# One 8 MB load of K per head, with half of it copied on-chip to free its slot, in a decode kernel with a long KV cache

## The chip, the cores and the metric

The kernel runs on one core of a Trainium2 chip; the other cores are idle. The metric is the device time of one execution in microseconds (us), as the median of several executions.

## The reference, cut to what matters

A decode step for two sequences: attention with 32 query heads on 4 KV heads over a cache of 32768 positions, then a small MLP. Everything is bf16.

```python
B, Sq, D = (2, 1, 1024)
Hq, Hkv, Sk, Dh = (32, 4, 32768, 128)
k = jnp.repeat(k_cache, rep, axis=1)           # k_cache, v_cache: [2, 4, 32768, 128]
v = jnp.repeat(v_cache, rep, axis=1)
scores = jnp.einsum('bhqd,bhkd->bhqk', q, k) * Dh ** (-0.5)
p = _softmax(scores, axis=-1)
o = jnp.einsum('bhqk,bhkd->bhqd', p, v)
# ... output projection wo, layernorm with modulation, MLP (w1 1024x3584, w2 3584x1024)
```

Each of the eight pairs of sequence and KV head ("a head" below, numbered 0 to 7) has 8.39 MB of K and 8.39 MB of V, read once. With the weights this makes 178 MB.

## The kernel before

PE is TensorE, PSUM the memory that its results go to here, and to evict is to copy from there to the on-chip memory that the loads fill (SBUF, 128 partitions). For each head, PE transposes K in 128x128 blocks into PSUM, VectorE and ScalarE evict these, PE multiplies them with q, a softmax over all 32768 scores follows, and only then can the product with V begin. All loads are issued by SyncE (SP) in program order. SP waits before each load until its slot in a 160 KB ring (per partition) is free.

```python
CH_ROWS = 8192          # a quarter of a head
TPC = CH_ROWS // 128    # 64 transposes per quarter, in 8 groups of 8
NCH = S // CH_ROWS      # 4 quarters
RING = 160 * 1024
EVAC_PATTERN = ("dve", "act", "dve", "act", "dve", "dve", "act", "dve")
# ...
def add_k(i, hf):       # half a head: 4 MB, 32 KB in each partition
    add(("K", i, hf), [2, TPC * D], A_k_cache[i % 2, i // 2].rearrange("(p h c t) d -> h p c (t d)", h=2, c=2, p=128)[hf], hf * 32 * KB, f"K{hf}")
def add_v(i):           # a whole head: 8 MB, 64 KB in each partition
    add(("V", i), [NCH, TPC * D], A_v_cache[i % 2, i // 2].rearrange("(p c t) d -> p c (t d)", c=NCH, p=128), 64 * KB, "V")
# ... stream of loads: wmod, wq, then for each head K half 0, K half 1, V, then wo, w1, w2
def need(*key):         # issues all loads up to this one, each after the readers of its slot
    # ...
        T.dma("sp", lambda e, dst=dst, src=cur.src: e.dma_start(dst, src), key=cur.sem, writes=[cur.reg], frees=old)
# ...
def tr(i, cc, g8):      # group g8 of quarter cc: 8 transposes, one eviction
    it = need("K", i, cc // 2)
    kt = it.view[:, cc % 2, :].rearrange("p (t d) -> p t d", d=D)
    # ... 8 x pe.transpose(psKT[g8 % 4], ...), then tensor_copy on VectorE or activation(Copy) on ScalarE
# ... for each head:
for cc in range(NCH):
    for g8 in range(TPC // 8):
        tr(i, cc, g8)
        pipe.append((i, cc, g8))
        # ...
        if len(pipe) > PIPE:
            qk(*pipe.pop(0))
# ... softmax, then pv(i, cc): the product with V; its last quarter frees V's slot
```

So the ring holds two K slots of 32 KB, one V slot of 64 KB and 32 KB that stay free during the heads. The first half of the next head's K can be loaded once half of this head's K has been transposed. The head loop is a hardware loop on PE, VectorE and ScalarE.

## Time and profile before

| | before |
|---|---|
| median of 3 runs | 419.99 us (419.98 to 420.0) |
| span of the profiled run | 418.7 us |
| moved from HBM | 178.28 MB |

The first fence has lines of the profile's page of the kernel before. The first line is busy time, share of the span and number of instructions by engine. PEclk and DMA are tenths in 40 equal slices of the span (9 is 90% or more), and GB/s is what the 16 DMA engines moved in each slice.

```profile
PE 291.0 (70%) x5183; PEld 231.3 (55%) x5183; DVE 209.6 (50%) x423; ACT 149.4 (36%) x179; POOL 6.8 (2%) x29
...
PEclk9999557986896997799589958986697889576585
DMA  9989999999999999999999999999999999899995
GB/s 373 450 380 449 448 404 493 398 406 446 441 432 429 423 451 429 419 454 457 391 435 476 407 416 448 438 438 426 438 438 426 416 460 457 377 448 428 424 427 249
DMA packets 5581, 178.42 MB, mean 426 GB/s; under 512 B 698, under 2 KB 706, under 8 KB 964
...
q8 instruction: 8, 0.13, 0.1%
...
DMA 71%; PE 24%; DVE 2%; issue 1%; ACT 1%; SPq 1%
```

DMA engines are busy in every slice, at 426 GB/s on average, and no compute engine comes near. The last line (the chain of waits that ended last) is mostly DMA. The trace's record of every DMA packet (a piece of a load that one of the 16 DMA engines moves at a time) says the same more sharply: between 20 us and 400 us the 16 engines together lack less than 0.05 us of work (the sum of their idle times, divided by 16). A 32 KB packet takes 1213 ns in the median and a 64 KB packet 2418. The latter is 27.1 GB/s on one engine, 434 GB/s on sixteen; the Trainium skill, "DMA: Bandwidth & Descriptors", section "Where 436 GB/s comes from", puts the ceiling of the path into SBUF at 435 GB/s, and this trace agrees. There is no room but in the number of bytes, in the cost per packet, and in the few us at both ends.

The next fence is the timeline of the DMA queue's issuer in the kernel before: start, time, queue, line, what was loaded (x2 is two issues merged, the second one later).

```profile
74.49 15.95 SPq L389 DMA_DIRECT2D K<-in_A_k_cache_dram  x2
102.47 0.33 SPq L389 DMA_DIRECT2D V<-in_A_v_cache_dram  x1
...
137.97 0.33 SPq L389 DMA_DIRECT2D V<-in_A_v_cache_dram  x1
...
174.92 0.33 SPq L389 DMA_DIRECT2D V<-in_A_v_cache_dram  x1
```

The V load at 102.47 us is that of head 1, into the slot that head 0's V has just left. By the packet records, the K of head 1 before it in the queue has its last byte at 110.6 us, and the first engine is through with it at 108.9. The issue leads by 6.4 us. In later heads it leads by more: that of head 3 is issued at 174.92, and the first engine is through with the K before it at 186.3.

Head 0 is slower than the others. Its PE timeline (start, time, then in brackets the idle time before and what ended it):

```profile
62.45 3.59 PE L536 MATMUL psKT<-ident,K 128*128 128x128 bf16 x32 [4.60 <-DMA K<-in_A_k_cache_dram]
...
77.35 0.22 PE L548 MATMUL psZ<-qcur,KT_sb 128*128 128x8 bf16 x3 [1.49 <-issue]
...
84.88 0.25 PE L548 MATMUL psS<-qcur,KT_sb 128*128 128x8 bf16 x4 [2.24 <-issue]
...
95.90 6.52 PE L584 MATMUL psZ<-V,E_sb 128*32 128x512 bf16 x64 [1.64 <-ACT E_sb L572]
```

K's first half is there at 62.45 us; two gaps called "issue" (PE waited for nothing that the profile knows) cost 1.49 and 2.24 us; the product with V starts at 95.90 and takes 6.5.

The windows of the same trace (columns: stretch, its length, busy time and count of PE, weight loads, VectorE, ScalarE and GpSimd, PE's clock, share of the DMA engines, GB/s):

```profile
core 0: us, PE busy (x) PEld busy (x) DVE busy (x) ACT busy (x) POOL busy (x), PEclk, DMA share, GB/s
90.00:110.00 20.00, 14.34 (x183) 9.29 (x181) 12.02 (x27) 6.86 (x9) 0.44 (x2) 0.74 1.02 437
110.00:115.00 5.00, 5.00 (x128) 5.00 (x126) 3.59 (x6) 3.45 (x4) 0.00 (x0) 1.00 0.97 419
115.00:135.00 20.00, 16.01 (x342) 13.83 (x342) 14.48 (x27) 11.47 (x15) 0.00 (x0) 0.85 0.99 428
```

And the eviction on VectorE, for its cost (busy time of the group, mean of one in ns, idle time before it):

```profile
L542 DVE COPY KT_sb<-psKT 128x1024 bf16<-128x1024 bf16 x160 | 106.7, 688 | 61.6 <-PE psKT L536 61.2
```

### The profile page before, as it was taken

The numbers are of one execution on the slowest core, as the hardware profiler recorded it, in microseconds if no ns is written. First come the engines' busy times: TensorE is split into PE (matmuls) and PEld (weight loads), VectorE is DVE, ScalarE is ACT, GpSimd is POOL, SyncE is SP. The second block draws the span as 40 slices with busy tenths as digits, with TensorE's granted clock in tenths as the row PEclk, the third lists the DMA queues.
The fourth block names the chain that finished last, engine by engine and source line by source line (L and its number), as shares of the span: only waits on it lengthen the run. The fifth ranks groups of instructions, "written<-read, shape, count | busy, mean of one in ns | idle before, by whom it ended". The sixth has DMA issues, their size and how long they took to land.

```text
span 418.7 us, 11609 instructions
## 1 busy us (share of the span) xinstructions
PE 291.0 (70%) x5183; PEld 231.3 (55%) x5183; DVE 209.6 (50%) x423; ACT 149.4 (36%) x179; POOL 6.8 (2%) x29
## 2 busy tenths in 40 slices
PE   1407449766996895699369957976995699564536
PEld 1104219762993794299149926962894399221214
DVE  1201105546677676467726664766477567620411
ACT  2000015533565364256405632643365166400100
POOL 3000000000000000000000000000000000000000
PEclk9999557986896997799589958986697889576585
DMA  9989999999999999999999999999999999899995
GB/s 373 450 380 449 448 404 493 398 406 446 441 432 429 423 451 429 419 454 457 391 435 476 407 416 448 438 438 426 438 438 426 416 460 457 377 448 428 424 427 249
DMA packets 5581, 178.42 MB, mean 426 GB/s; under 512 B 698, under 2 KB 706, under 8 KB 964
## 3 DMA queue, kind: packets, MB, share of 16 engines
q1 hardware_dynamic: 5572, 178.28, 98.8%
q8 instruction: 8, 0.13, 0.1%
q14 instruction: 1, 0.01, 0.0%
HBM read 178.28 MB, written 0.00 MB: 426 GB/s over the span
## 4 chain that ended last, share of the span: by engine, by line
DMA 71%; PE 24%; DVE 2%; issue 1%; ACT 1%; SPq 1%
DMA V<-in_A_v_cache_dram 39%; DMA wo<-in_A_wo_dram 10%; DMA K<-in_A_k_cache_dram 10%; PE psZ L584 10%; DMA w<-in_B_w_dram 9%; PE psKT L536 8%; DMA wmod<-in_w_mod_dram 4%; PE psS L548 1%; PE psZ L548 1%; PE psS L655 1%; PE psZ L729 1%; PE psZ L469 1%; ACT KT_sb L540 0%; PE psS L469 0%; DVE m1c L553 0%
## 5 line engine op out<-in xcount | busy, mean ns | idle before, releaser
L536 PE MATMUL psKT<-ident,K 128*128 128x128 bf16 x2048 | 163.1, 229 | 11.5 <-DMA K<-in_A_k_cache_dram 11.5
L540 ACT ACTIVATE KT_sb<-psKT 128x1024 bf16<-128x1024 bf16 x96 | 98.2, 1025 | 124.4 <-PE psKT L536 124.4
L542 DVE COPY KT_sb<-psKT 128x1024 bf16<-128x1024 bf16 x160 | 106.7, 688 | 61.6 <-PE psKT L536 61.2
L536 PEld LDWEIGHTS psKT<-ident,K 128*128 128x128 bf16 x2048 | 126.7, 102 | 13.0 <-DMA K<-in_A_k_cache_dram 12.7
L584 PE MATMUL psZ<-V,E_sb 128*32 128x512 bf16 x512 | 46.4, 541 | 23.2 <-DMA V<-in_A_v_cache_dram 20.0
L548 PE MATMUL psS<-qcur,KT_sb 128*128 128x8 bf16 x1024 | 44.7, 167 | 2.2 <-issue 2.2
L584 PEld LDWEIGHTS psZ<-V,E_sb 128*32 128x32 bf16 x512 | 18.7, 130 | 47.7 <-issue 38.8
L548 PE MATMUL psZ<-qcur,KT_sb 128*128 128x8 bf16 x1024 | 43.0, 167 | 2.2 <-issue 1.5
L548 PEld LDWEIGHTS psS<-qcur,KT_sb 128*128 128x128 bf16 x1024 | 40.0, 97 | 2.3 <-issue 2.3
L548 PEld LDWEIGHTS psZ<-qcur,KT_sb 128*128 128x128 bf16 x1024 | 37.9, 96 | 3.4 <-issue 1.6
L572 ACT ACTIVATE E_sb<-S_sb 128x512 bf16<-128x512 f32 x32 | 19.5, 630 | 29.6 <-DVE S_sb L570 29.6
L570 DVE TENSOR_TENSOR S_sb<-S_sb,gmb 128x512 f32<-128x512 f32 x32 | 20.0, 685 | 0.3
L576 DVE TENSOR_REDUCE rs<-E_sb 128x8 f32<-128x512 bf16 x32 | 19.7, 675 | 0.0
L469 PE MATMUL psS<-wmod,inT 128*32 128x512 bf16 x32 | 5.1, 624 | 16.2 <-DMA wmod<-in_w_mod_dram 16.2
L553 DVE TENSOR_REDUCE m1c<-psZ 128x8 f32<-128x512 f32 x16 | 11.1, 693 | 10.2 <-ACT S_sb L552 10.1
L595 DVE RECIPROCAL rinv<-psM 128x1 f32<-128x1 f32 x8 | 1.3, 168 | 27.7 <-PE psM L593 27.7
L605 PE MATMUL psM<-msum,hmat 128*128 128x128 f32 x16 | 4.2, 347 | 13.3 <-DVE msum L600 13.3
L559 PE MATMUL psM<-identf,m 128*8 128x128 f32 x16 | 4.3, 369 | 13.1 <-DVE m L556 13.1
L553 DVE TENSOR_REDUCE m1c<-psS 128x8 f32<-128x512 f32 x16 | 11.1, 693 | 3.2 <-ACT S_sb L552 3.1
L552 ACT ACTIVATE S_sb<-psZ 128x512 f32<-128x512 f32 x16 | 9.5, 595 | 7.5 <-PE psZ L548 7.5
L477 DVE COPY S_sb<-psS 128x512 f32<-128x512 f32 x1 | 0.7, 690 | 22.9 <-PE psS L469 22.9
L469 PEld LDWEIGHTS psS<-wmod,inT 128*32 128x32 bf16 x32 | 1.1, 132 | 19.3 <-DMA wmod<-in_w_mod_dram 18.0
(123 smaller groups left out, 167.5 us busy)
## 6 DMA issues: line engine op xcount, KB each, us to landing
K<-in_A_k_cache_dram SPq DMA_DIRECT2D x16, 4096.0 KB, 27.1
wq<-in_A_wq_dram SPq DMA_DIRECT2D x2, 4096.0 KB, 44.8
wo<-in_A_wo_dram SPq DMA_DIRECT2D x2, 4096.0 KB, 39.0
w<-in_B_w_dram SPq DMA_DIRECT2D x2, 3584.0 KB, 32.5
wmod<-in_w_mod_dram SPq DMA_DIRECT2D x1, 6144.0 KB, 29.8
w<-in_B_w_dram SPq DMA_DIRECT2D x3, 2048.0 KB, 37.8
wmod<-in_w_mod_dram SPq DMA_DIRECT2D x1, 4608.0 KB, 15.8
wmod<-in_w_mod_dram SPq DMA_DIRECT2D x1, 1536.0 KB, 6.0
```

The source lines that it names most:

```text
L469: pe(lambda e, w=it.view, k=k, kk=kk, ch=ch, n=n, q=q: e.matmul(bank[n][32 * q:32 * q + 32, :], lhsT=inT[:, k, :], rhs=w[:, kk, ch * 512:( ...
L536: pe(lambda e, kq=kq, jj=jj, w=kt, t=t: e.transpose(psKT[kq][:, jj * 128:(jj + 1) * 128], w[:, t, :], ident[:, :]), reads=[it.reg, "ident" ...
L540: act(lambda e, src=src: e.activation(KT_sb[g8][:, :, :], src, ACT.Copy), reads=[f"psKT{kq}"], writes=[f"KT_sb{g8}"], sem=f"ev{cc}_{g8}")
L542: dve(lambda e, src=src: e.tensor_copy(KT_sb[g8][:, :, :], src), reads=[f"psKT{kq}"], writes=[f"KT_sb{g8}"], sem=f"ev{cc}_{g8}")
L548: pe(lambda e, t=t, jj=jj: e.matmul(ps[:, t * HPG:(t + 1) * HPG], lhsT=KT_sb[g8][:, jj, :], rhs=qcur[:, :], start=True, stop=True), reads= ...
L552: act(lambda e: e.activation(Sc, ps.rearrange("p (t h) -> p h t", h=HPG), ACT.Copy), reads=[preg], writes=[f"S_sb_{cc}"], sem=f"sc{cc}")
L553: dve(lambda e: e.tensor_reduce(m1c[:, :, cc], ps.rearrange("p (t h) -> p h t", h=HPG), AX.X, ALU.max), reads=[preg], writes=[f"m1c{cc}"])
L559: pe(lambda e: e.matmul(psM[0:HPG, 0:128], lhsT=m1[:, :], rhs=identf[:, :], start=True, stop=True), reads=["m1", "identf"], writes=["psM"])
L570: dve(lambda e: e.tensor_tensor(Sc, Sc, gmb[:, :].unsqueeze(2).to_broadcast([128, HPG, TPC]), ALU.subtract), reads=[f"S_sb_{cc}", "gmb"], ...
L572: act(lambda e: e.activation(Ec, Sc.rearrange("p h (u t) -> p u h t", t=4), ACT.Exp, scale=SCALE), reads=[f"S_sb_{cc}"], writes=[f"E_sb_{c ...
L576: dve(lambda e: e.tensor_reduce(rs4[:, :, cc], Ec.rearrange("p u h t -> p h u t"), AX.XY, ALU.add), reads=[f"E_sb_{cc}"], writes=[f"rs4_{c ...
L584: pe(lambda e, t4=t4, tg=tg, q=q: e.matmul(psO[32 * q:32 * q + 32, :], lhsT=E_sb[:, tg // 4, :, :].rearrange("p h t -> p (h t)"), rhs=vt[: ...
```

## The change

The intent: K's packets become as large as V's, a single load and semaphore per head replace two, and the second half of K is copied to the spare 32 KB early in the head (with copies on VectorE, which was half idle), so that the slot is free again at half time as before. The eviction pattern shifts some work to ScalarE in the first two quarters, and the weights after the heads move within the ring.

```diff
--- before
+++ after
@@
 RING = 160 * 1024
+KC_AT = 128 * 1024
 AHEAD = ("sc2", "sc3", "pk", "ac")
 WMOD_ITEMS = ((0, 1), (1, 4), (4, 8))
-W2_ITEMS = ((0, 8, 96), (8, 16, 112), (16, 24, 128), (24, 27, 144), (27, 28, 150))
-EVAC_PATTERN = ("dve", "act", "dve", "act", "dve", "dve", "act", "dve")
+W2_ITEMS = ((0, 8, 96), (8, 16, 112), (16, 24, 0), (24, 27, 16), (27, 28, 22))
+EVAC_PATTERN = (("dve", "act") * 4, ("dve", "act", "dve", "act", "dve", "dve", "act", "dve"))
@@
-    def add_k(i, hf):
-        add(("K", i, hf), [2, TPC * D], A_k_cache[i % 2, i // 2].rearrange("(p h c t) d -> h p c (t d)", h=2, c=2, p=128)[hf], hf * 32 * KB, f"K{hf}")
+    def add_k(i):
+        add(("K", i), [NCH, TPC * D], A_k_cache[i % 2, i // 2].rearrange("(p c t) d -> p c (t d)", c=NCH, p=128), 0, "K")
@@
     for i in range(NBG):
-        add_k(i, 0)
-        add_k(i, 1)
+        add_k(i)
         add_v(i)
-    for m, off in enumerate((128, 0)):
+    for m, off in enumerate((0, 32)):
         add(("wo", m), ...)
-    for m, off in enumerate((32, 64)):
+    for m, off in enumerate((128, 64)):
         add(("w1", m), ...)
@@
+    kc = nc.alloc_sbuf_tensor_at("kc", [128, 2, TPC * D], BF16, offset=abase + KC_AT)
@@ need
+            if cur.n > by_key["V", NBG - 1].n and cur.off < KC_AT + 32 * KB and KC_AT < cur.off + cur.nbytes:
+                old += [f"kc{n}" for n in range(4)]
@@ before the heads
+    T.wait("dve", writes=[it.reg for it in stream if it.key[0] in ("wmod", "wq")])
@@ tr
-        it = need("K", i, cc // 2)
-        kt = it.view[:, cc % 2, :].rearrange("p (t d) -> p t d", d=D)
+        it = need("K", i)
+        kt = (it.view[:, cc, :] if cc < 2 else kc[:, cc - 2, :]).rearrange("p (t d) -> p t d", d=D)
+        k_reg = it.reg if cc < 2 else f"kc{2 * (cc - 2) + g8 // 4}"
@@
-               reads=[it.reg, "ident"], writes=[f"psKT{kq}"], mark=(jj == 7))
+               reads=[k_reg, "ident"], writes=[f"psKT{kq}"], mark=(jj == 7))
@@
-        if EVAC_PATTERN[g8] == "act":
+        if EVAC_PATTERN[cc // 2][g8] == "act":
@@
+    def keep(i, n):
+        it = need("K", i)
+        lo = n % 2 * 32 * D
+        dve(lambda e: e.tensor_copy(kc[:, n // 2, lo:lo + 32 * D], it.view[:, 2 + n // 2, lo:lo + 32 * D]), reads=[it.reg], writes=[f"kc{n}"], sem=f"kc{n}")
@@ head loop
                 tr(i, cc, g8)
+                if cc < 2 and g8 % 4 == 1:
+                    keep(i, 2 * cc + g8 // 4)
```

## The prediction

> **What bounds it now.** The DMA engines. The page gives 178.42 MB in a span of 418.7 us (426 GB/s), and its row of DMA tenths is 9 nearly everywhere; windows by stage show a DMA share near 1 in every head. The packet records show all 16 engines without a gap from about 4 us to 414 us. PE is busy 70%. From the third head on, the chain of waits is "DMA V" of 31 to 33 us, then 5 to 6 us of second matmul. The next load is always issued early: in head 0 the DMA queue's timeline has the next V issued at 102.47 us, while K's last packet ends at 110.7; in later heads the lead is some 13 us.
>
> **What changes.**
> 1. K packets double to 64 KB. By the packet records a 32 KB packet takes 1213 ns, a 64 KB packet (V) 2418: 8 ns saved of 2426. K has 2048 small packets: 1024 x 8 ns / 16 engines = 0.5 us in all. The Trainium skill, "DMA: Bandwidth & Descriptors", "Why small descriptors are slow", has a fixed cost per packet; the trace agrees: 0.3% here.
> 2. Four VectorE copies of 128x4096 bf16 a head, SBUF to SBUF. No such copy is in the trace. The Trainium skill, "VectorE: DVE Perf Modes", "Side-by-side", gives four elements a cycle at 0.96 GHz plus about 150 cycles: an estimate of 1.23 us each, 4.9 us a head, 39 us in all (VectorE 50% to about 59%). The measured 688 ns of a 1024-element PSUM eviction fit the formula at two a cycle. Some evictions move to ScalarE (1025 ns). The first half of a head then needs about 11.8 us of VectorE (8 evictions, 4 copies, 2 maxima) against 9.1 to 12 us measured: 0 to 1.5 us slower, off the critical path in later heads.
> 3. One semaphore for 8 MB: transposes start when all of K is there, 9.7 us later than the first half was. The next K is still queued in time, but V's slot is freed about 9.5 us later relative to the DMA stream. In later heads transposes, softmax and second matmul take about 32 us from K's landing, against 38.7 us of DMA: 5 us or so to spare.
>
> **Where it hurts: head 0.** There the work from K's landing (62.45) to V's release (102.47) takes 40 us ("issue" gaps of 1.5 and 2.2 us in the chain; a half clock at the start). With K landing at about 71.8, V's slot is freed at about 112.5, data flow again 1 us later (first load: issued 0.74, first packet 1.8), and K of head 1 is through at about 110.5. The queue runs dry once, for about 3 us; nothing makes that up. The tail is unchanged.
>
> **Predicted:** 420.0 - 0.5 + 3 = 422.5 us; 80% range 419.5 to 426. Faster by over 2%: 0.01; within 2%: 0.96; slower by over 2%: 0.03.
>
> **What would show it.** K in 1024 packets of 64 KB at about 2418 ns; copies near 1.2 us; one dip in the DMA row near 110 us, with V of head 1 issued after K of head 1 landed; DMA share near 1 elsewhere.
>
> **What would make it wrong.** Head 0 running faster when it starts later (no gap: 419.5); copies in a slower mode (2.3 us each would stretch every head and open gaps in head 1 too, 426 or more); instruction fetches queued behind larger packets.

## The result, and the profile after

| | before | after |
|---|---|---|
| median of 6 runs | 420.01 us (419.98 to 420.09) | 424.63 us (422.76 to 427.97) |
| ratio of fast runs, 95% interval | | 1.0113 (1.0074 to 1.0151) |
| profiled run | 420.02 us, span 418.7 | 427.97 us, span 426.7 |

A ratio is the mean time of one kernel's fast runs over the mean of the other's in the same rounds, so it is not quite the ratio of the medians. The change made the kernel 1.1% slower, and its runs now differ by 5 us, where those of before differ by 0.1. The profiled run of after is its slowest one; its numbers show the mechanism at its largest.

The page of the kernel after:

```profile
PE 296.1 (69%) x5183; PEld 236.6 (55%) x5183; DVE 232.5 (54%) x439; ACT 166.2 (39%) x195; POOL 6.8 (2%) x29
...
PEclk9976565887689678966988896799669789969555
DMA  9999999999499999999999999999999999999995
GB/s 369 442 418 432 418 475 399 475 413 439 155 393 405 479 393 492 393 461 424 393 492 393 479 405 399 485 393 492 393 442 442 393 492 393 437 405 441 419 433 228
DMA packets 4429, 178.42 MB, mean 418 GB/s; under 512 B 570, under 2 KB 578, under 8 KB 836
...
q8 instruction: 8, 0.13, 0.1%
...
DMA 60%; PE 34%; DVE 2%; issue 2%; ACT 1%; SPq 0%
```

There is one hole in the DMA row, a 4 in the eleventh slice, with 155 GB/s in it. All other slices up to the last are full. K's packets are fewer (4429 packets in all, from 5581), VectorE has 23 us more, ScalarE 17.

The DMA queue's issuer after:

```profile
36.92 0.33 SPq L392 DMA_DIRECT2D K<-in_A_k_cache_dram  x1
...
84.38 0.33 SPq L392 DMA_DIRECT2D K<-in_A_k_cache_dram  x1
115.18 0.33 SPq L392 DMA_DIRECT2D V<-in_A_v_cache_dram  x1
...
150.75 0.33 SPq L392 DMA_DIRECT2D V<-in_A_v_cache_dram  x1
...
190.98 0.33 SPq L392 DMA_DIRECT2D V<-in_A_v_cache_dram  x1
```

K of head 0 is one load now (issued at 36.92), so the transposes wait until all of it is down, at 72 us, and V of head 1 is issued at 115.18. By the packet records the K before it ended at 110.6, as it did in the kernel before. The first packet of V follows at 116.1. The windows show the hole directly:

```profile
core 0: us, PE busy (x) PEld busy (x) DVE busy (x) ACT busy (x) POOL busy (x), PEclk, DMA share, GB/s
90.00:110.00 20.00, 12.86 (x233) 11.14 (x235) 10.57 (x19) 7.94 (x11) 0.00 (x0) 0.76 0.89 380
110.00:115.00 5.00, 5.00 (x56) 1.72 (x44) 2.43 (x6) 1.59 (x2) 0.00 (x0) 0.55 0.00 0
115.00:135.00 20.00, 18.23 (x388) 17.90 (x385) 16.38 (x27) 12.02 (x13) 0.44 (x2) 0.91 1.00 419
```

From 110 to 115 us the DMA engines moved nothing. PE's timeline of head 0 after:

```profile
72.26 3.60 PE L541 MATMUL psKT<-ident,K 128*128 128x128 bf16 x32 [14.27 <-DMA K<-in_A_k_cache_dram]
...
87.30 0.22 PE L558 MATMUL psZ<-qcur,KT_sb 128*128 128x8 bf16 x3 [1.85 <-issue]
...
97.01 0.24 PE L558 MATMUL psS<-qcur,KT_sb 128*128 128x8 bf16 x4 [3.14 <-issue]
...
108.55 6.57 PE L594 MATMUL psZ<-V,E_sb 128*32 128x512 bf16 x64 [1.65 <-ACT E_sb L582]
```

The groups of VectorE after: evictions, and the new copies.

```profile
L547 DVE COPY KT_sb<-psKT 128x1024 bf16<-128x1024 bf16 x144 | 96.6, 686 | 65.6 <-PE psKT L541 65.6
...
L552 DVE COPY kc<-K 128x4096 bf16<-128x4096 bf16 x32 | 38.9, 1216 | 0.0
```

The packet records give the loss stage by stage. Each line but the last is the time by which the 16 engines together had moved all bytes up to and including a load, in us from the start, in the two profiled runs:

```
                     before    after   difference
K of head 0           70.49    70.53     +0.04
V of head 0           90.09    89.95     -0.15
K of head 1          109.61   110.41     +0.80
V of head 1          128.93   136.40     +7.47
V of head 7          361.02   368.34     +7.31
w1                   397.43   404.90     +7.47
w2, all but its end  414.01   421.43     +7.42
last byte            415.49   423.37     +7.88
```

All of the loss in the heads arises by the end of V of head 1. From there to V of head 7 the kernel after is 0.16 us faster, and the weights cost 0.1 us. At the very end the last engine lags 0.5 us more than before. (By the last byte of each load the weights seem to cost 1.3 us. That is one late engine: the last packets of w1 ended between 404.7 and 405.1 us on most engines, but one at 406.19.)

### The profile page after: what moved, and what is told of

It is laid out like the page before. It is cut to its first block, busy times and chain, and to the rows that moved or that the text cites. A ratio compares the mean times of both kernels' runs of the same rounds, so it can differ in the third digit from the quotient of the medians.

```text
span 426.7 us, 11649 instructions
## 1 busy us (share of the span) xinstructions
PE 296.1 (69%) x5183; PEld 236.6 (55%) x5183; DVE 232.5 (54%) x439; ACT 166.2 (39%) x195; POOL 6.8 (2%) x29
## 2 busy tenths in 40 slices
DMA packets 4429, 178.42 MB, mean 418 GB/s; under 512 B 570, under 2 KB 578, under 8 KB 836
## 4 chain that ended last, share of the span: by engine, by line
DMA 60%; PE 34%; DVE 2%; issue 2%; ACT 1%; SPq 0%
DMA K<-in_A_k_cache_dram 45%; PE psKT L541 22%; DMA w<-in_B_w_dram 8%; DMA wmod<-in_w_mod_dram 7%; PE psS L558 3%; PE psZ L594 3%; PE psZ L558 3%; PE psZ L472 1%; PE psZ L741 1%; DVE msum L610 1%; ACT KT_sb L545 0%; PE psS L667 0%; PE psS L472 0%; DVE m1c L563 0%; DVE S_sb L580 0%
## 5 line engine op out<-in xcount | busy, mean ns | idle before, releaser
L545 ACT ACTIVATE KT_sb<-psKT 128x1024 bf16<-128x1024 bf16 x112 | 114.8, 1025 | 122.7 <-PE psKT L541 122.7
L547 DVE COPY KT_sb<-psKT 128x1024 bf16<-128x1024 bf16 x144 | 96.6, 686 | 65.6 <-PE psKT L541 65.6
L541 PE MATMUL psKT<-ident,K 128*128 128x128 bf16 x1024 | 89.7, 246 | 28.6 <-DMA K<-in_A_k_cache_dram 28.5
L541 PEld LDWEIGHTS psKT<-ident,K 128*128 128x128 bf16 x1024 | 72.4, 112 | 30.2 <-DMA K<-in_A_k_cache_dram 29.9
L541 PE MATMUL psKT<-ident,kc 128*128 128x128 bf16 x1024 | 80.2, 222 | 0.0
L541 PEld LDWEIGHTS psKT<-ident,kc 128*128 128x128 bf16 x1024 | 60.1, 99 | 0.0
L594 PE MATMUL psZ<-V,E_sb 128*32 128x512 bf16 x512 | 45.0, 529 | 13.2 <-ACT E_sb L582 13.2
L558 PEld LDWEIGHTS psS<-qcur,KT_sb 128*128 128x128 bf16 x1024 | 41.1, 99 | 3.2 <-issue 3.2
L552 DVE COPY kc<-K 128x4096 bf16<-128x4096 bf16 x32 | 38.9, 1216 | 0.0
L594 PEld LDWEIGHTS psZ<-V,E_sb 128*32 128x32 bf16 x512 | 16.8, 128 | 38.2 <-issue 20.1
```

The lines of the kernel that those rows point to most:

```text
L541: pe(lambda e, kq=kq, jj=jj, w=kt, t=t: e.transpose(psKT[kq][:, jj * 128:(jj + 1) * 128], w[:, t, :], ident[:, :]), reads=[k_reg, "ident"] ...
L545: act(lambda e, src=src: e.activation(KT_sb[g8][:, :, :], src, ACT.Copy), reads=[f"psKT{kq}"], writes=[f"KT_sb{g8}"], sem=f"ev{cc}_{g8}")
L547: dve(lambda e, src=src: e.tensor_copy(KT_sb[g8][:, :, :], src), reads=[f"psKT{kq}"], writes=[f"KT_sb{g8}"], sem=f"ev{cc}_{g8}")
L552: dve(lambda e: e.tensor_copy(kc[:, n // 2, lo:lo + 32 * D], it.view[:, 2 + n // 2, lo:lo + 32 * D]), reads=[it.reg], writes=[f"kc{n}"], s ...
L558: pe(lambda e, t=t, jj=jj: e.matmul(ps[:, t * HPG:(t + 1) * HPG], lhsT=KT_sb[g8][:, jj, :], rhs=qcur[:, :], start=True, stop=True), reads= ...
L594: pe(lambda e, t4=t4, tg=tg, q=q: e.matmul(psO[32 * q:32 * q + 32, :], lhsT=E_sb[:, tg // 4, :, :].rearrange("p h t -> p (h t)"), rhs=vt[: ...
```

## The experiments

Theory A, the prediction's: the kernel is bound by DMA, each head has a few us between the release of V's slot and the end of the K load ahead in the queue, and only head 0 uses that time up, because its transposes start 9.7 us later. Rival B: the copies on VectorE cost time in every head. Rival C: the 64 KB packets of K cost time by themselves, for example by holding up instruction fetches, which go through the same DMA engines (in the records of both kernels only 15 engines move data while a fetch runs in mid-stream). Eleven kernels were run; all gave correct results.

### e3_before_wait: the late start alone, in the kernel before

```diff
 # kernel before, tr()
-               reads=[it.reg, "ident"], writes=[f"psKT{kq}"], mark=(jj == 7))
+               reads=[it.reg, "ident"] + ([need("K", i, 1).reg] if cc < 2 else []), writes=[f"psKT{kq}"], mark=(jj == 7))
```

> The kernel before (no copies, 32 KB packets, two K slots), with one edit: the transposes of the first half of K wait for the second half's load too. A: the late start alone makes the dry spell in head 0, 423 to 425 us, and no loss in later heads. B and C: 420.0, as the kernel before.

Measured: 424.72 us (422.50 to 426.58), ratio 1.0107 (1.0083 to 1.0131). V of head 1 in its issuer's timeline:

```profile
110.48 0.33 SPq L389 DMA_DIRECT2D V<-in_A_v_cache_dram  x1
```

With no copy, no larger packet and one wait more (in every head, as in the changed kernel), a loss of the same size is there, with a similar spread. Neither B nor C is needed for it. But it is not made up in the same way. In this kernel's packet records the DMA engines lack 1.4 us of work at 110 to 113 us and 0.2 at 99 to 101, and slow packets add 2.6 us more than in the kernel before (below, "The size of the loss"). By bytes moved it is 2.8 us behind the kernel before at the end of V of head 1, and 4.3 at the end: 1.6 us are lost in later stages, where A expected nothing. What slows packets there was not tested.

### e2_split_wait: the changed kernel with 32 KB packets, late start kept

```diff
 # kernel after, need(): K as two loads with a semaphore each, region it.reg + "b" for the second half
+            if cur.key[0] == "K":
+                T.dma("sp", ... e.dma_start(dst[:, 0:2, :], src[:, 0:2, :]), key="d_K", writes=[cur.reg], frees=old)
+                T.dma("sp", ... e.dma_start(dst[:, 2:4, :], src[:, 2:4, :]), key="d_Kb", writes=[cur.reg + "b"])
 # tr() and keep() read both regions
```

> As e1_split, with 32 KB packets, but the transposes of the first half and all copies wait for the second 4 MB load too. A: the late start is back, so 424 to 426 us, V of head 1 issued 3 to 6 us after K of head 1 landed. C (packet size): 420 to 420.5. B: near 424.6.

Measured: 423.81 us (422.36 to 424.90), ratio 1.0084 (1.0068 to 1.0101). This is just under the expected 424. V of head 1 was issued at 110.46 us, about when K of head 1 ended and not 3 to 6 us later, and the queue lacked 1.9 us of work. Packets of 32 KB keep most of the loss, so C as the main cause falls. That this run is 0.8 us under the changed kernel is within the spread of both.

### e1_split: two loads again, meant to start early

```diff
 # as e2_split_wait, but tr() of quarters 0 and 1 reads it.reg alone and keep() reads it.reg + "b" alone
```

> The changed kernel with each head's K as two 4 MB loads again (32 KB packets, a semaphore for each half, transposes start on the first half); slot, gate for the next K, copies and eviction pattern stay. Theory A (all of the loss is one dry spell of the DMA queue in head 0, because V's slot there is freed after the next K has landed): no dry spell, V of head 1 issued near 105 us, 420.0 +- 0.5 us. Rival B (the copies slow the kernel): stays near 424.6. Rival C (the 64 KB packets of K themselves slow it, by delaying instruction fetches or by slower packets): 420 as well, so this run doesn't tell A from C.

Measured: 422.92 us (420.32 to 423.47), ratio 1.0058 (1.0037 to 1.0079); V of head 1 issued at 108.55. The expectation of 420.0 missed. The experiment had a flaw: the first copy stands on VectorE behind the first group's eviction, and it waits for the second load. In VectorE's timeline the copy runs at 72.14 us, 8 us after the eviction before it, and the next evictions only at 73.29, so PE stood still until 74 us after six groups. The run did half of what it was for, and the loss fell by over a third. The same flaw is in the next one, where its line is shown.

### e4_head0: only head 0's K in two loads

```diff
 # as e1_split, but with
+            if cur.key[0] == "K" and cur.key[1] == 0:      # else one 8 MB load that writes both regions
 # (the wait for d_Kb in the loop is on a constant)
```

> The changed kernel with K of head 0 alone as two 4 MB loads with a semaphore each; heads 1 to 7 keep one 8 MB load with 64 KB packets and the copies. A: no dry spell, and K's larger packets are left as the only difference: 419.5 to 420.0 us, seven eighths of the 0.5 us under the kernel before. B and C: most of the loss stays, 423.5 to 424.6, since seven heads of eight are as changed.

Measured: 422.02 us (420.56 to 423.78), ratio 1.0050 (1.0031 to 1.0068); 419.5 to 420.0 was expected, so this missed too. The issue of V of head 1, and PE's timeline of head 0:

```profile
107.20 0.33 SPq L399 DMA_DIRECT2D V<-in_A_v_cache_dram  x1
```

```profile
62.75 3.60 PE L548 MATMUL psKT<-ident,K 128*128 128x128 bf16 x32 [4.62 <-DMA K<-in_A_k_cache_dram]
...
74.28 0.37 PE L565 MATMUL psS<-qcur,KT_sb 128*128 128x8 bf16 x8 [6.19 <-DVE KT_sb L554]
```

PE starts at 62.75 and stands from 68 to 74.28 for an eviction on VectorE that is behind a copy. V of head 1 was issued at 107.20, 8 us before that of the changed kernel's profiled run, and the queue lacked only 0.2 us. More than half of the loss is gone by a change to head 0 alone, with seven heads as in the changed kernel. That speaks against B and C. But an issue at 107.2 is close to the edge (the first engine is through with K at about 109, and data come 1.0 us after an issue), and the timed runs spread over 3 us.

### e7_head0_late and e8_late: copies later in the head

```diff
+KEEP_AT = ((1, 3), (1, 5), (1, 7), (2, 1))
-                if cc < 2 and g8 % 4 == 1:
-                    keep(i, 2 * cc + g8 // 4)
+                if (cc, g8) in KEEP_AT:
+                    keep(i, KEEP_AT.index((cc, g8)))
 # e7: on top of e4_head0; e8: on the changed kernel
```

> As e4_head0 (only head 0's K in two loads), and the four copies of a head moved later: after the groups 3, 5, 7 of the second quarter and 1 of the third, so that in head 0 VectorE no longer waits for the second load in front of the first evictions. (In e4_head0 PE stood 6.2 us at 68 to 74 us for that.) Theory A (one dry spell in head 0, set by when V is released there): V of head 1 issued at 103 to 106 us, no dry spell, 419.5 to 420.0 us in all rounds, spread under 0.5. Rival B (the copies cost time in every head): 422 or more, as seven heads are as changed.

> The control of e7_head0_late: the changed kernel with the copies moved in the same way and one 8 MB load in every head. A: the late start is there, so the dry spell too: 423 to 426 us. If the place of the copies were what matters (a form of B): 420.

Measured: e7_head0_late 430.34 us (428.93 to 432.02), ratio 1.0256 (1.0233 to 1.0278). e8_late 431.66 us (428.55 to 435.02, one of six runs slow), ratio of the fast ones 1.0248 (1.0222 to 1.0275). Both expectations missed by far. The issuer's timeline of e7 and its windows:

```profile
97.87 0.33 SPq L400 DMA_DIRECT2D V<-in_A_v_cache_dram  x1
128.02 0.33 SPq L400 DMA_DIRECT2D K<-in_A_k_cache_dram  x1
```

```profile
126.00:134.00 8.00, 7.46 (x182) 7.14 (x180) 7.28 (x12) 4.96 (x6) 0.00 (x0) 1.00 0.82 328
```

Head 0 did what was hoped for: V of head 1 was issued at 97.87. But there is a second deadline in each head. K's slot is freed by the last copy, and the next K must be issued before V of this head is down. The four copies, bunched between evictions, ended so late that K of head 2 was issued at 128.02, when the engines ran out of V, at 128.0 to 130. From 126 to 134 us the DMA share is 0.82. The packet records show seven such holes of 0.1 to 1.2 us after that point in e7, and seven of 0.4 to 1.7 us in e8, from 89 us on; five of e7's seven stand in front of a load into K's slot (K or wo), two in front of a V. The holes are less than half of the loss: 4.0 of 9.2 us in e7 and 5.6 of 12.3 in e8, by bytes moved. Slow packets (below) are the larger part, 5.5 and 7.0 us. So copies can cost time in every head: not by their work on VectorE, which is the same, but by when they free the slot. In the kernel after they are early enough: no hole after head 1.

### e5_twice: every copy made twice

```diff
 # kernel after, keep()
+        dve(lambda e: e.tensor_copy(kc[...], it.view[...]), reads=[it.reg], writes=[f"kc{n}"], sem=f"kd{n}")
         dve(lambda e: e.tensor_copy(kc[...], it.view[...]), reads=[it.reg], writes=[f"kc{n}"], sem=f"kc{n}")
```

> The changed kernel with every copy made twice (39 us of VectorE more, 4.9 us a head). A: heads 1 to 7 have about 4 us between V's release and the landing of the next K, head 0 has none, so head 0 pays what the copies stretch its first half by (0 to 4 us) and the others pay under 1 us each: 425 to 430 us, V of head 1 issued at 115 to 119 us. B (copies cost in every head one for one): a stretch of some 3 us in each of eight heads, 440 or more.

Measured: 435.58 us (433.63 to 437.57), ratio 1.0377 (1.0351 to 1.0402). It lies between the two expectations, and V of head 1 was issued at 111.16, not at 115 to 119. The packet records have eight holes of 0.3 to 2.0 us, from head 0 on, 7.6 us in all with the smallest ones, and 7.3 us more in slow packets, so the time to spare in later heads is less than the 4.9 us of added copies plus the second of issue. The copies as they are (4.9 us a head) leave no hole after head 1; twice as many leave one in front of every V from head 1 on. What A expected of the later heads (under 1 us each) was too little.

### e6_v0_small and e10_before_v0: V of head 0 in small packets

```diff
 # need(), in the changed kernel (e6) and in the kernel before (e10)
+            if cur.key == ("V", 0):
+                for p in range(NCH):     # four 2 MB loads, 16 KB packets, one semaphore
+                    T.dma("sp", ... e.dma_start(dst[:, p, :], src[:, p, :]), key=cur.sem, writes=[cur.reg] if p == NCH - 1 else [], frees=old if p == 0 else [])
```

> The changed kernel with V of head 0 as four 2 MB loads with 16 KB packets on the same semaphore. Instruction fetches go through the same DMA engines; PE's issue gaps in head 0 (1.85 us at 85 us and 3.14 us at 94 us) follow fetches that waited behind 64 KB packets. If so, the gap at 85 us, which falls in V's load, shrinks by about 1 us and V of head 1 is issued as much earlier: 423.3 to 424.3 (the smaller packets cost 0.2 us themselves). If the gaps don't come from waiting behind packets: 424.6 as before, gap unchanged.

> The kernel before with the one edit of e6_v0_small: V of head 0 as four 2 MB loads with 16 KB packets. If the instruction fetches' wait behind packets is what e6_v0_small took away, PE's issue gaps in head 0 (1.5 and 2.2 us) shrink here too and V of head 1 is issued 2 to 5 us before 102.5; but in this kernel that load is early anyway, so the time doesn't fall: 420.0 to 420.4 (0.2 for the smaller packets).

Measured: e6_v0_small 422.36 us (421.11 to 425.04), ratio 1.0065 (1.0043 to 1.0087), lower than expected. e10_before_v0 420.14 us (420.07 to 420.26), ratio 1.0004 (0.9990 to 1.0017). PE's timelines of head 0, first e6, then e10:

```profile
72.28 3.29 PE L546 MATMUL psKT<-ident,K 128*128 128x128 bf16 x32 [14.32 <-DMA K<-in_A_k_cache_dram]
...
90.97 0.24 PE L563 MATMUL psS<-qcur,KT_sb 128*128 128x8 bf16 x4 [1.09 <-issue]
```

```profile
83.06 0.24 PE L553 MATMUL psS<-qcur,KT_sb 128*128 128x8 bf16 x4 [1.42 <-issue]
```

In both kernels the first issue gap is gone (1.85 us in the changed kernel, 1.49 in the one before) and the second is smaller (1.09 from 3.14, 1.42 from 2.24). V of head 1 was issued at 107.17 in e6 and at 99.93 in e10, 2.5 us earlier than in the kernel before. In the changed kernel this took 2.3 us of the median away (the two were not timed in the same rounds, and the intervals of their ratios overlap a little; e9_head0_v0 beside e4_head0 below shows the same, 420.49 against 422.02); in the kernel before, where that load is early anyway, it changed nothing. Fetches show as queue q8 on the page, 8 packets of 16 KB; the second gap of the changed kernel (93.87 to 97.01) contains one at 94.7 to 95.7. The Trainium skill, "Runtime: NRT & Kernel Launch", section "Instruction fetch mechanics", says that an engine's sequencer fetches blocks of 16 KiB through its own DMA queue and that the cost is mostly hidden; "DMA: Bandwidth & Descriptors", section "Queues, rings and completion order", that a DMA engine changes between queues only at packet boundaries (its packets are groups of descriptors, the single transfers that a load is split into; whether a 64 KB record is one such packet is not shown here). The runs agree with the blocks of 16 KB on a queue of their own, not with "mostly hidden", and fit the waiting for a packet's end without showing it directly: here fetches behind 64 KB packets came with gaps of up to 3.1 us. The gaps differ much between runs: e2_split_wait had 0.48, 1.97 and 0.33 us, and e5_twice and e8_late, where VectorE held PE up, had none. The first gap was also gone in e7_head0_late and e11_head0_spread, where V of head 0 kept its 64 KB packets but VectorE had held PE up for 1.2 and 1.9 us before. So small packets are not all that takes a gap away, and each kernel was profiled once. The gaps make the size of the hole vary, and could be the source of the new spread; the spread itself was not taken apart.

### e9_head0_v0 and e11_head0_spread: head 0 mended

```diff
 # e9:  e4_head0 with the edit of e6_v0_small
 # e11: e4_head0 with
+KEEP_AT = ((0, 6), (1, 1), (1, 4), (1, 7))
```

> e4_head0 and e6_v0_small together: K of head 0 in two loads, V of head 0 in 16 KB packets; heads 1 to 7 as changed. Theory A, with the instruction fetches as what sets the size of the dry spell: V of head 1 issued before 106 us in every run, no dry spell, 419.7 to 420.2 us with a spread under 0.6. If larger packets or the copies cost time in the other seven heads: 421.5 or more.

> e4_head0 with the copies after group 6 of the first quarter and groups 1, 4 and 7 of the second: late enough that head 0's evictions wait little for the second load, early and spread enough that later heads free K's slot at least 3 us before V lands (the miss of e7_head0_late). A: V of head 1 issued at 99 to 105 us, no dry spell anywhere, 419.6 to 420.1 us. If it goes above 421.5, look for a late K issue in heads 1 to 7.

Measured: e9_head0_v0 420.49 us (420.23 to 421.66), ratio 1.0021 (1.0007 to 1.0034). e11_head0_spread 421.34 us (420.12 to 422.60), ratio 1.0024 (1.0010 to 1.0037). For e9, the issue of V of head 1, and the window that was empty in the changed kernel:

```profile
105.52 0.33 SPq L403 DMA_DIRECT2D V<-in_A_v_cache_dram  x1
```

```profile
110.00:115.00 5.00, 3.86 (x43) 3.86 (x44) 2.42 (x3) 1.25 (x2) 0.00 (x0) 0.50 0.97 419
```

The hole is gone, and with it over four fifths of the loss (0.5 us by medians and 0.9 by the ratio over its own runs of before, where the changed kernel was 4.6 and 4.7 over), while seven heads of eight keep the single loads and the large packets, and all keep the copies, the new eviction pattern and the moved weights. e11 was issued in time too (104.16), but still lost 0.15 and 0.12 us in two later heads and 1.1 us more than the kernel before to slow packets. Both ended above what was expected, and neither beats the kernel before. What keeps e9 at 0.5 us above it, rather than 0.3 below, is not found: its profiled run (420.29 us) is within 0.1 us of the kernel before at every load, by bytes moved, and its slower runs were not profiled.

### The size of the loss

The profiled runs of these kernels line up by when V of head 1 was issued. The hole is what the 16 engines together lacked near 110 us, from the packet records. "Slow" is the time by which data packets took longer than the median of their size in the kernel before, over the whole run, divided by 16, less the 0.91 us that the kernel before has itself.

```
kernel             V issued   hole us   slow us   profiled run us
e10_before_v0         99.93     0.00     -0.07         420.16
before               102.47     0.00      0            420.02
e9_head0_v0          105.52     0.00      0.08         420.29
e6_v0_small          107.17     0.09      0.97         421.11
e4_head0             107.20     0.22      0.53         420.83
e1_split             108.55     0.55      1.10         422.58
e3_before_wait       110.48     1.37      2.62         425.02
e2_split_wait        110.46     1.91      1.17         423.96
after                115.18     6.75      0.91         427.97
```

Up to about 105 us the issue time doesn't matter; beyond 107 the time rises with it. (e11_head0_spread, issued at 104.16 with no hole here, had 422.60 us in its profiled run; its losses were elsewhere, as told. e5, e7 and e8 have holes in many heads and don't belong in this table.) It rises by more than the hole where the hole is small, and slow packets are most of the difference: hole and slow packets together come within 1.1 us of the loss in every line. When the queue starts again, the first packet on nearly every engine is slow. In the kernel after, 15 of the first 16 packets, from 116.1 us on, took 2773 to 3414 ns instead of 2418, together worth 0.7 us; the first 16 in e2 and e3 lost 0.7 us too. Why packets are slow there, and why others are far from any hole (e3), was not tested.

## Why the prediction was right

The time (422.5 predicted, 424.63 measured, range 419.5 to 426) and the mechanism held. Point by point:

- **DMA is the bound, and K's packets give 0.5 us.** The bound is right, the gain about half. There are 1024 more packets of 64 KB, still at 2418 ns in the median. But from the first packet of a K to the first of the V after it (heads 2 to 7) pass 19.36 us in the kernel before and 19.32 to 19.33 in the one after: 0.035 us a head, some 0.3 us in eight, or 4 ns a packet and not 8. Eight 64 KB packets pass in 19.32 us, 2415 ns each, where their records say 2418, and sixteen of 32 KB in 19.36, 1210 each, where they say 1213: the records overlap a little, and the sum of their durations is too large.
- **The copies take 1.23 us each and lie off the critical path.** Right for the kernel after: 1216 ns in the profile. VectorE rose to 54%, not 59%, since evictions moved to ScalarE and the span grew. In head 0 the first two quarters took no longer than before.
- **Some 5 us to spare in later heads.** Somewhat too much, but enough: V of head 3 was issued at 190.98 and PE had the K before it at 195.05, so 4.1 us; the first engine was through with that K at 194.12, so 3.1 us by the measure used above, of which 1.0 goes to the start of the transfer.
- **One dry spell in head 0, nothing makes it up.** Right, shown by the stage table, by e3_before_wait (the late start alone gives a loss of the same size, though only 2.8 of its 4.3 us by the end of V of head 1) and by e9_head0_v0 (mending head 0 takes most of it away).
- **The size, "V's slot is freed at about 112.5 ... for about 3 us".** This term was too small for the profiled run. V was issued at 115.18 and the last engine was dry for 5.5 us. From K's landing to V's release head 0 took 42.9 us instead of 40.0: 1.3 us more of issue gaps, the rest from half-clock stretches after the gaps (from the first gap to the end of the scores PE's granted clock was 0.80 instead of 0.88) and in the softmax (0.62 instead of 0.91). One cost was left out of the sum: slow packets (0.9 us, of which 0.7 when the queue starts again). "The tail is unchanged" held to 0.1 us in bytes moved, with a last engine that ended 0.5 us later. The median run lost 4.6 us where 2.5 were predicted; no run near the median was profiled, so its hole isn't known.
- **Instruction fetches as a risk.** Named only as something that might go wrong; the small-packet runs suggest that they set part of the size.

## What to carry to other kernels

Where DMA bounds a kernel, judge a change by the lead of each load: the time from its issue (plus the start of its data, 1.0 us here) to the end of what is ahead of it in the queue. A single large load saves little (some 0.3 us here) and moves the start of work to its end (9.8 us later here), so look at the first, slow iteration of a loop, which has the smallest lead. An on-chip copy that frees a slot sets a second deadline: moving it by a few groups cost 7 us here although its work stayed the same.

## What the Trainium skill lacked or had wrong

- "DMA: Bandwidth & Descriptors", "Why small descriptors are slow", deals with packets of some hundred bytes. Here the cost per packet at 32 to 64 KB was 2 x 1213 - 2418 = 8 ns by the packets' durations, but only 4 ns by the pace of the stream (0.035 us for 8 packets fewer on each engine).
- No page that was read says that a queue that has run dry starts slowly: the first 64 KB packets took 2773 to 3414 ns instead of 2418 on 15 of 16 engines.
- "DMA: Bandwidth & Descriptors", "Specifications", gives a first-byte latency of about 0.6 us for loads issued by SP. From the start of the issue (0.33 us long) to the first packet it was 0.96 us here, so 0.63 from its end: it agrees, but a lead must cover the sum.
- "Runtime: NRT & Kernel Launch", "Instruction fetch mechanics", calls the cost of crossing a 16 KiB block mostly hidden. In the first pass of the loop, behind 64 KB packets, PE had gaps of 1.5 to 3.1 us in the kernels before and after; with 16 KB packets one of two was gone.
- "VectorE: DVE Perf Modes", "Side-by-side", was right for a size that it doesn't list: 1.23 us by its formula for 128x4096 bf16, 1216 ns measured.
